# Second feed-forward products as 384 and 192 columns, with the feed-forward steps in the order in which the program traces them

## The chip, the core and the metric

The kernel runs on one core of a Trainium2 chip. A core has five engines with a queue each: TensorE (PE: matrix products, and PEld: the weight loads that go before each product), VectorE (DVE), ScalarE (ACT), GpSimd (POOL) and SyncE (SP, used for DMA issues alone). An engine works through its queue in order, and waits on semaphores for the others. Products write to PSUM, which has eight banks of 128 partitions x 512 float32; everything else works from SBUF.

The metric is the time of the program on the device in microseconds, the median of the runs shown.

## The reference, cut to what matters

Inputs are A_u (1, 2048, 576), the parameters of a state-space convolution (576 channels, 128 states), and the weights w1 (576, 4608) and w2 (4608, 576), all float32.

```
xn  = layernorm(A_u)
ssm = irfft(rfft(xn, 4096) * rfft(K, 4096))[:2048] + xn * Dskip
      K[d, l] = Re sum_n C[d,n] * dt[d] * B[d,n] * exp(dt[d] * A[d,n] * l)
ffn = silu(xn @ w1) @ w2
out = A_u + ssm + ffn
```

The change lies in `ffn`, and there in the second product, `silu(xn @ w1) @ w2`, and in the order of both products on TensorE.

## The kernel before, in words

**Precision.** A float32 product is made of three products of rounded parts (float32r): each operand is split into a high and a low part, and high x high, high x low and low x high are summed in PSUM. ScalarE makes the high part by a copy that rounds, VectorE the low part by a subtraction.

**Feed-forward tiling (`ffn`).** The 2048 tokens are two halves of two blocks of 512. The 4608 hidden units are nine chunks of four tiles of 128. The loop runs over 36 blocks: half, chunk, block of 512 tokens. For a block, `up` (from line 321) computes a tile of 128 hidden units x 512 tokens: 14 products of 512 columns (12 on line 331, one each on lines 332 and 333), then Silu into `gf`, a rounding copy `gh` and the rest `gl` (lines 339 to 342). `down` (from line 344) computes 128 tokens x 576 outputs: the weights of TensorE are 128 tokens of `gh` or `gl`, the moving operand is a part of `w2`. The 576 columns go as two halves of 288 (`HD`), each in a PSUM bank `po` of its own, with 4 tiles x 3 products = 12 products on line 357. After a half VectorE adds the bank to the accumulator `acc[j]` (line 361). There are 144 such steps (36 blocks x 4), with 24 products and two adds each.

**Order.** The program is traced block by block: `u0` of the next block, `d0` to `d3` of this one, `u1`, `u2`, `u3` of the next (the loop over steps at the end of `ffn`), and loads and splits of the next chunk's weights in between (`after`). The order traced is not the order of an engine's queue: a scheduler with a timeline of its own places instructions, and so products of `up` and `down` stand mixed on TensorE. `behind(ins)` (a helper over `tc.issue_after`) tells it to place what follows after an instruction; `tc.high_priority()` puts the adds and the Silu ahead of other work.

**The rest** (`side`, woven between the feed-forward steps by `weave` at shares of the whole): layer norm and transposes of the first 1024 tokens at the start (`phase0`, `normed`, `put_xt`: four transposes a tile on line 124, a copy `xh` on line 125, a subtraction `xl` on line 126; lines 132 to 135 for the last 64 channels), parameters (`natural`), the table of the convolution kernel (`kgen`, VectorE's lines 630 to 676, TensorE's lines 696 and 711, with `spread`, lines 157 to 163), the spectral part (`spectral`, lines 750 to 826), and the inverse (`tail`, `add_conv`, line 847). `marks` (line 865) has the shares at which these begin and end: 0.13 to 0.597 for `kgen`, 0.597 to 0.823 for `spectral`.

**Banks.** PSUM has three pools: `ps1` (two banks) for `up`, `ps2` (three) for `down` and one bank of `add_conv`, `pss` (three) for everything else.

**Weights.** `split_w2` (line 308) loads nothing; it makes `w2h` and `w2l`, each a tile [128, 576] of its own with five buffers, from the loaded `w2r`.

**Start.** Block 0's ups run as two halves of 256 tokens, so that the first 256 tokens are enough to begin; TensorE is kept at work with products of zeros (`idle`, line 879) until then. Tokens 512 to 1023 (block 1, tiles 4 to 7) are normalised and transposed after that.

## Time and profile before

| | |
|---|---|
| median of three runs | 1111.25 us (1109.95 to 1111.63) |
| profiled execution, span from first to last instruction | 1108.2 us |
| profiled execution with what lies around its span | not recorded apart; the median of the runs is 3.05 us above the span |
| TensorE busy (products / weight loads) | 1102.2 us (99%) / 997.5 us (90%) |
| VectorE / ScalarE busy | 916.6 us (83%) / 706.9 us (64%) |
| chain that ended last | TensorE 98%: line 357 42%, line 331 35% |
| granted TensorE clock, mean | 1.000 |

How to read it: a row of a timeline has the start in us from the span's beginning, the time that the merged instructions took together, engine, line of the kernel, operation, tiles written <- tiles read, shape of the weights (TensorE) and of what is written, and how many were merged (x4). In square brackets stands idle time of the engine before it and who ended it. A row of the chain has start, length and the number of instructions. A row of waits has who waited for whom: us in total, times, the longest. Products overlap one another, so a product's own duration (0.29 us for 288 columns) is longer than its distance to the next. An average over the span hides that its stages differ: in slices 6 to 22 of 40 VectorE works on the table of `kgen`, later on the spectral part.

### The profile page before, as it was taken

How to read it: one execution, taken by the hardware profiler on the slowest of the kernel's cores; microseconds unless marked ns; L12 is line 12 of the kernel's file. 1: busy time of each engine (PE TensorE's matmuls, PEld its weight loads, DVE VectorE, ACT ScalarE, POOL GpSimd, SP SyncE). 2: the span in 40 equal slices, each digit the busy share in tenths (PEclk: the TensorE clock that was granted, in tenths of full speed). 3: DMA queues.
4: the chain of work that ended last, by engine and by line, in shares of the span. 5: the costliest groups of instructions: out<-in, count | busy, mean ns of one | idle time of the engine just before them, and what ended most of it. 6: DMA issues, size and time to landing. Idle time of an engine off the chain costs nothing.

```text
span 1108.2 us, 22917 instructions
## 1 busy us (share of the span) xinstructions
PE 1102.2 (99%) x9167; PEld 997.5 (90%) x9167; DVE 916.6 (83%) x1543; ACT 706.9 (64%) x1222; POOL 72.1 (7%) x129
## 2 busy tenths in 40 slices
PE   9999999999999999999999999999999999999998
PEld 7989998899998899899999989999999999999887
DVE  7799899999999999999999737787778778784433
ACT  4564466676677676677867536877777878774210
POOL 1100000000000000011000000000000000000111
PEclk9999999999999999999999999999999999999999
DMA  9745512525252525264744173554544455434983
GB/s 270 190 123 160 152 50 61 120 73 131 77 121 83 116 72 118 77 174 154 206 122 103 45 179 109 162 167 123 156 145 152 138 149 170 129 107 127 241 224 87
DMA packets 175755, 148.56 MB, mean 134 GB/s; under 512 B 111088, under 2 KB 142592, under 8 KB 175520
## 3 DMA queue, kind: packets, MB, share of 16 engines
q1 hardware_dynamic: 165328, 112.63, 38.7%
q0 software_dynamic: 9568, 33.62, 9.6%
q8 instruction: 72, 1.18, 0.5%
q10 hardware_dynamic: 752, 0.85, 0.3%
q14 instruction: 35, 0.29, 0.1%
HBM read 102.53 MB, written 44.61 MB: 133 GB/s over the span
## 4 chain that ended last, share of the span: by engine, by line
PE 98%; DMA 1%; DVE 1%; SPq 0%; issue 0%; DVEq 0%
PE po L357 42%; PE ph L331 35%; PE kp L696 3%; PE ph L332 3%; PE ph L333 3%; PE pu L826 2%; PE pb L826 2%; PE pk L826 2%; PE z L711 2%; PE pu L161 1%; PE py L847 1%; DMA acc<-in_A_u_dram 1%; PE pu L162 1%; PE pt L124 0%; DVE w1l L295 0%; PE ptk L490 0%
## 5 line engine op out<-in xcount | busy, mean ns | idle before, releaser
L357 PE MATMUL po<-w2l,gh 128*128 128x288 f32 x1152 | 338.5, 295 | 0.0
L357 PE MATMUL po<-w2h,gl 128*128 128x288 f32 x1152 | 336.4, 295 | 0.0
L357 PE MATMUL po<-w2h,gh 128*128 128x288 f32 x1152 | 336.1, 295 | 0.0
L357 PEld LDWEIGHTS po<-w2h,gh 128*128 128x128 f32 x1152 | 215.2, 188 | 7.7 <-issue 2.8
L357 PEld LDWEIGHTS po<-w2l,gh 128*128 128x128 f32 x1152 | 215.9, 188 | 5.1 <-issue 0.5
L357 PEld LDWEIGHTS po<-w2h,gl 128*128 128x128 f32 x1152 | 215.4, 188 | 0.9
L339 ACT ACTIVATE gf<-ph 128x512 f32<-128x512 f32 (+1 forms) x148 | 86.4, 584 | 143.8 <-PE ph L333 134.8
L331 PE MATMUL ph<-xh,w1l 128*128 128x512 f32 (+1 forms) x592 | 161.3, 385 | 0.0
L331 PE MATMUL ph<-xh,w1h 128*128 128x512 f32 (+1 forms) x592 | 161.3, 387 | 0.0
L331 PE MATMUL ph<-xl,w1h 128*128 128x512 f32 (+1 forms) x592 | 161.1, 385 | 0.0
L361 DVE TENSOR_TENSOR acc<-po,acc 128x288 f32<-128x288 f32 x288 | 126.2, 451 | 37.0 <-PE po L357 35.6
L342 DVE TENSOR_TENSOR gl<-gf,gh 128x512 fp32r<-128x512 f32 (+1 forms) x148 | 99.0, 672 | 64.6 <-ACT gh L340 63.8
L331 PEld LDWEIGHTS ph<-xh,w1l 128*128 128x128 f32 x592 | 108.0, 188 | 20.0
L331 PEld LDWEIGHTS ph<-xl,w1h 128*128 128x128 f32 x592 | 107.9, 188 | 19.8
L331 PEld LDWEIGHTS ph<-xh,w1h 128*128 128x128 f32 x592 | 104.5, 188 | 16.7 <-ACT x L133 0.5
L340 ACT CAST gh<-gf 128x512 fp32r<-128x512 f32 (+1 forms) x148 | 89.5, 608 | 9.5 <-PE po L357 6.6
L653 ACT ACTIVATE c<-th,magic 128x1040 f32<-128x1040 f32 x36 | 42.1, 1168 | 37.9 <-DVE C L676 28.0
L655 ACT ACTIVATE c<-th 128x1040 f32<-128x1040 f32 x36 | 38.7, 1075 | 33.6 <-DVE th L654 33.6
L314 ACT CAST w2h<-w2r 128x576 fp32r<-128x576 f32 x72 | 47.0, 671 | 17.7 <-PE po L357 14.9
L295 DVE TENSOR_TENSOR w1l<-w1r,w1h 128x640 fp32r<-128x640 f32 x72 | 56.9, 817 | 0.2
L332 PE MATMUL ph<-x,w1h 128*128 128x512 f32 (+1 forms) x148 | 57.0, 386 | 0.0
L333 PE MATMUL ph<-x,w1l 128*128 128x512 f32 (+1 forms) x148 | 56.9, 385 | 0.0
(185 smaller groups left out, 1828.8 us busy)
## 6 DMA issues: line engine op xcount, KB each, us to landing
w2r<-in_B_w_dram SPq DMA_DIRECT2D x72, 288.0 KB, 3.8
w1r<-in_B_w_dram SPq DMA_DIRECT2D x35, 512.0 KB, 3.8
d1u<-u POOLq DMA_DIRECT2D x32, 288.0 KB, 2.5
d1k<-stage SPq DMA_DIRECT2D x18, 512.0 KB, 6.8
ur<-d1u SPq DMA_DIRECT2D x32, 288.0 KB, 3.7
kr<-d1k SPq DMA_DIRECT2D x32, 288.0 KB, 2.9
d<-yo POOLq DMA_DIRECT2D x32, 288.0 KB, 4.0
ys<-d SPq DMA_DIRECT2D x32, 288.0 KB, 11.8
```

The source lines that it names most:

```text
L295: pins["w1l"] = nc.vector.tensor_sub(l1, src, h1).ins
L314: pins["w2h"] = nc.scalar.copy(h2, r2).ins
L331: nc.tensor.matmul(ph, w[:, kt, :], v[:, kt, a:e], start=n + kt == 0, stop=False)
L332: nc.tensor.matmul(ph, h1[:, 4, :], x4[:, a:e], start=False, stop=False)
L333: pins["pe"] = nc.tensor.matmul(ph, l1[:, 4, :], x4[:, a:e], start=False, stop=True).ins
L339: nc.scalar.activation(gf, ph, AF.Silu)
L340: pins["gh"] = nc.scalar.copy(gh, gf).ins
L342: pins["gl"] = nc.vector.tensor_sub(gl, gf, gh).ins
L357: pins["pe"] = nc.tensor.matmul(po[:, :HD], G[blk, t][g][:, js], W2[half, c, t][w][:, hs], start=n == 0, stop=n == 3 * FT - 1).ins
L361: nc.vector.tensor_add(acc[j][:, hs], po[:, :HD], acc[j][:, hs])
L653: nc.scalar.activation(c65, th, AF.Identity, bias=magic)
L826: nc.tensor.matmul(dst, st, mv[:, hs], start=n == 0, stop=n == 3 * len(terms) - 1)
```

## The change

*Columns.* `DA` = 384 and `DB` = 192 take the place of two halves of 288. The first bank of a step takes 12 products of 384 columns. The second bank takes, for each of four tiles, one product of 2 x 192 columns with `gh` as weights: the last 192 columns of the high and of the low part of w2 side by side (so that high x high lands in columns 0 to 191 and high x low in 192 to 383 of the bank), and one of 192 columns with `gl` as weights, which adds low x high to the first 192. On the last tile the two change places. VectorE then makes three adds: 384 columns, and twice 192 into the same columns of `acc`. High and low parts of w2 lie in one tile `w2s` [128, 2, 576] for this.

*Order.* An `up` of whole width is placed behind the last product of the step traced before it (`pins["pe"]`); a step's products for the first bank are placed behind the last product of the step before (`head`), those for the second bank behind the end of the first (`end`). The half-width ups of block 0 keep their rules.

*Marks.* The table work of `kgen` ends, and `spectral` begins, at a share of 0.612 in place of 0.597.

```diff
--- before.py
+++ after.py
@@ -25,6 +25,8 @@
 NJ = 16
 NKT = 4
 HD = D // 2
+DA = 384
+DB = D - DA
 NFT = FF // P
 MAGIC = 12582912.0
 TWO_PI = float(np.nextafter(np.float32(2 * math.pi), np.float32(0)))
@@ -308,15 +310,15 @@
         def split_w2(half, c, t):
             first = half == 0 and c == 0
             r2 = R2.pop((half, c, t))
-            h2 = wp.tile([P, D], F32R, tag="w2h", name="w2h", bufs=FT + 1)
-            l2 = wp.tile([P, D], F32R, tag="w2l", name="w2l", bufs=FT + 1)
+            hl = wp.tile([P, 2, D], F32R, tag="w2s", name="w2s", bufs=FT + 1)
+            h2, l2 = hl[:, 0], hl[:, 1]
             with behind(pins["xt_s"] if first else pins["gh"]):
                 pins["w2h"] = nc.scalar.copy(h2, r2).ins
             with behind(pins["w1l"] if first else None):
                 pins["w2l"] = nc.vector.tensor_sub(l2, r2, h2).ins
             if first and t == 0:
                 pins["w2l0"] = pins["w2l"]
-            W2[half, c, t] = h2, l2
+            W2[half, c, t] = hl
 
         def up(blk, t, a=0, e=512, after=None):
 
@@ -325,6 +327,8 @@
             h1, l1 = W1[half, c, t]
             pool, tag = (ps2, "ps2") if e == 256 and t > 1 else (ps1, "ps1")
             ph = pool.tile([P, 512], F32, tag=tag, name="ph")[:, a:e]
+            if after is None and a == 0 and e == 512:
+                after = pins["pe"]
             for n, (w, v) in enumerate(((h1, xh), (h1, xl), (l1, xh))):
                 for kt in range(NKT):
                     with behind(after):
@@ -348,17 +352,26 @@
             if half == 1 and c == NCH - 1:
                 if jj % 2 == 0:
                     add_conv(j, (acc[j], acc[j + 1]))
-            for h in range(2):
-                hs = slice(h * HD, (h + 1) * HD)
-                po = ps2.tile([P, 512], F32, tag="ps2", name="po")
-                n = 0
-                for t in range(FT):
-                    for g, w in ((0, 0), (0, 1), (1, 0)):
-                        pins["pe"] = nc.tensor.matmul(po[:, :HD], G[blk, t][g][:, js], W2[half, c, t][w][:, hs],
-                                                      start=n == 0, stop=n == 3 * FT - 1).ins
-                        n += 1
+            pa_, pb_ = (ps2.tile([P, 512], F32, tag="ps2", name="po") for _ in range(2))
+            parts = [(*(g[:, js] for g in G[blk, t]), W2[half, c, t], t == 0, t == FT - 1) for t in range(FT)]
+            head = pins["pe"]
+            for gh, gl, w, first, last in parts:
+                with behind(head):
+                    nc.tensor.matmul(pa_[:, :DA], gh, w[:, 0, :DA], start=first, stop=False)
+                    nc.tensor.matmul(pa_[:, :DA], gh, w[:, 1, :DA], start=False, stop=False)
+                    end = nc.tensor.matmul(pa_[:, :DA], gl, w[:, 0, :DA], start=False, stop=last).ins
+            with tc.high_priority():
+                nc.vector.tensor_add(acc[j][:, :DA], pa_[:, :DA], acc[j][:, :DA])
+            both = pb_[:, :2 * DB].rearrange("p (s d) -> p s d", s=2)
+            for gh, gl, w, first, last in parts:
+                with behind(end):
+                    mms = [lambda: nc.tensor.matmul(both, gh, w[:, :, DA:], start=first, stop=last),
+                           lambda: nc.tensor.matmul(pb_[:, :DB], gl, w[:, 0, DA:], start=False, stop=False)]
+                    for mm in mms[::-1] if last else mms:
+                        pins["pe"] = mm().ins
+            for o in (0, DB):
                 with tc.high_priority():
-                    nc.vector.tensor_add(acc[j][:, hs], po[:, :HD], acc[j][:, hs])
+                    nc.vector.tensor_add(acc[j][:, DA:], pb_[:, o:o + DB], acc[j][:, DA:])
             if half == 0 and c == NCH - 1:
                 rows = slice(j * P, (j + 1) * P)
                 nc.sync.dma_start(dr0[rows, :], acc[j])
@@ -862,7 +875,7 @@
 
     def side():
         nonlocal s4, kl, yp, pa, tail_at
-        marks = (0.13, 0.597, 0.823)
+        marks = (0.13, 0.612, 0.823)
         tail_at = (0.91, 0.934, 0.967, 0.0072)
         with tc.tile_pool(name="kf", bufs=1) as kfp:
             for n in ("f", "phi"):
```

## The prediction

> **What bounds the kernel now.** I read the page first (busy times, slices, the chain that ended last), then TensorE's list of waits, then its timeline where one form of product stands alone, and last the first 50 us and VectorE's stretch of kernel-table work.
>
> ```profile
> span 1108.2 us, 22917 instructions
> PE 1102.2 (99%) x9167; PEld 997.5 (90%) x9167; DVE 916.6 (83%) x1543; ACT 706.9 (64%) x1222; POOL 72.1 (7%) x129
> DVE  7799899999999999999999737787778778784433
> PE 98%; DMA 1%; DVE 1%; SPq 0%; issue 0%; DVEq 0%
> ...
> PEld po L357 <- issue: 3.3, 7, 0.5
> ...
> PEld kp L696 <- DVE acc L361: 1.7, 5, 0.4
> ...
> PEld po L357 <- DVE acc L361: 0.4, 1, 0.4
> ```
>
> TensorE is the chain: 98% of it. The waits of its weight loads are a few us in total, those on VectorE about 2 us. So a change is worth what it does to the distance from one product to the next, plus any gap that it opens. VectorE stands at nine tenths in slices 6 to 22, so it is the next bound there.
>
> **The price of a product.** The start of one product to the start of the next is what counts, not the duration of one.
>
> ```profile
> 663.03 3.18 PE po L357 x24
> ...
> 14.07 0.64 PE L331 MATMUL ph<-xh,w1h 128*128 128x256 f32 x4
> ...
> 15.50 0.64 PE L331 MATMUL ph<-xl,w1h 128*128 128x256 f32 x4
> ...
> 800.55 1.07 PE L331 MATMUL ph<-xl,w1h 128*128 128x512 f32 x4
> 801.46 1.07 PE L331 MATMUL ph<-xh,w1l 128*128 128x512 f32 x4
> ...
> 802.59 0.39 PE L333 MATMUL ph<-x,w1l 128*128 128x512 f32 x1
> 802.82 0.29 PE L357 MATMUL po<-w2h,gh 128*128 128x288 f32 x1
> ...
> 301.65 0.29 PE L357 MATMUL po<-w2h,gh 128*128 128x288 f32 x1
> ...
> 301.43 0.19 PEld L357 LDWEIGHTS po<-w2h,gh 128*128 128x128 f32 x1
> 301.65 0.19 PEld L357 LDWEIGHTS po<-w2l,gh 128*128 128x128 f32 x1
> ...
> 501.92 0.19 PEld L161 LDWEIGHTS pu<-sp,s 128*128 128x128 f32 x1
> 502.03 0.19 PEld L162 LDWEIGHTS pu<-sp,s 128*128 128x128 f32 x1
> ```
>
> 288 columns: 3.18/24 = 0.1325 us. 256 columns: 12 in 1.43 us = 0.1192. 512 columns: 4 in 0.91 us = 0.2275. From 288 to 512 that is 0.095/224 = 0.000424 us a column and 0.0104 us fixed; so 384 columns cost 0.1732, and 192, if columns alone counted, 0.0918. A step from one bank to another (802.59 to 802.82, 0.23) costs no more than a step inside one. Loads set a floor: at 501.92 two loads follow each other with nothing ahead of them, 0.11 apart, and only one is drawn ahead: the load for the second product of line 357 starts at 301.65, with the first product, and not when the load of 301.43 was over. A product of 192 columns is over before the next load is, so I price it at 0.11. Its bounds are 0.0918 (columns alone) and 0.1192 (the 256-column row, which a load cannot exceed); the two loads at 501.92 are the nearest row, since they show the load by itself.
>
> [...]
>
> **The change, part by part.**
>
> 1. *Second products.* A step (block, jj) had 24 products of 288: 24 x 0.1325 = 3.180. It now has 12 of 384, four of 384 (both 192s at once) and four of 192: 16 x 0.1732 + 4 x 0.11 = 3.211. 36 blocks x 4 are 144 steps: 144 x 0.031 = **+4.5 us**. Columns streamed are 6912 on both sides. With 192 at 0.0918 it is 144 x -0.042 = -6.0; at 0.1192, 144 x 0.068 = +9.8. That the moving operand of the joint product lies in two pieces has no row; between nothing and one more fixed 0.0104 for each of the 576, +6.0; I take nothing, since the products of one piece in other shapes all fit one line.
>
> 2. *The order written out, at the start.* In the built program TensorE's queue holds all eight half-width first products of block 0, then all 20 transposes of tokens 4 to 7, then up 0 of block 1, and only then the first second product. Before, those filled this time:
>
> ```profile
> 20.00:40.80 20.80, 14.03 (x96) 13.01 (x96) 1.00 0.81 242
> ...
> 30.53 0.29 PE L333 MATMUL ph<-x,w1l 128*128 128x256 f32 x1
> 30.66 0.60 PE L124 MATMUL pt<-ident,xn 128*128 128x128 f32 x4
> ...
> 40.82 2.00 PE L331 MATMUL ph<-xh,w1h 128*128 128x512 f32 x8
> ...
> 46.96 0.39 PE L333 MATMUL ph<-x,w1l 128*128 128x512 f32 x1
> ...
> 26.48 0.79 ACT L339 ACTIVATE gf<-ph 128x256 f32<-128x256 f32 x2 [2.88 <-DVE gl L342]
> ...
> 28.66 0.87 ACT L207 ACTIVATE xn<-acc,mb,sd 128x576 f32<-128x576 f32 x1 [0.80 <-POOL sd L198]
> ...
> 31.29 0.59 ACT L125 CAST xh<-pt 128x512 fp32r<-128x512 f32 x1
> ...
> 27.93 0.57 DVE L202 TENSOR_SCALAR xn<-acc,mv,sd 128x576 f32<-128x576 f32 x1
> ...
> 30.58 1.53 DVE L193 BATCH_NORM_STATS2 st<-xj 128x6 f32<-128x288 f32 x4
> ...
> 32.03 0.67 DVE L126 TENSOR_TENSOR xl<-pt,xh 128x512 fp32r<-128x512 f32 x1
> ...
> 37.65 0.77 DVE L250 STREAM_TRANSPOSE tr<-xj 128x576 f32<-128x576 f32 x1
> ...
> 40.28 0.42 DVE L135 TENSOR_TENSOR x<-pt,x 64x256 fp32r<-64x256 f32 x1
> ```
>
> (The first row is a window of line 357 alone: TensorE's busy time, products, loads, clock.) All 96 second products of block 0 lay between 20 and 40.8 us, and up 0 of block 1 began at 40.82, when its last operand (VectorE's line 135, 40.28 + 0.42) came. What of that chain stays: tokens 4 are normalised at 28.5 (27.93 + 0.57), 5 at 29.5 (28.66 + 0.87), whatever TensorE does. The last half-width up waits for its bank, which the Silu of 26.48 frees: it runs from about 26.9 to 28.6 (14 x 0.1192). Then each of four transposed tiles takes a copy of 0.59 and a subtraction of 0.67, through three banks, behind token 7's normalisation on ScalarE (0.87) and the 1.53 of statistics and other rows on VectorE; the adds of line 361 no longer stand between. Walking the queues by these durations: ScalarE has token 5 done at 29.5, the last Silu, token 7 at 30.6 and the first copy at 31.2; VectorE subtracts to 31.9, which frees the first of the three banks, so token 6's transposes end at 32.5 and its copy at 33.1; the second bank is free at 32.8, token 7's copy is done at 34.2. VectorE has a normalisation (0.57) and a turn (0.77) between, and so subtracts tokens 6 and 7 to 34.4 and 35.7 and the narrow rest to 36.1, 4.6 earlier than before. Up 0's first four products run meanwhile; its last ten end at 38.0. Then 4 steps x 3.211 and one up (14 x 0.2275 = 3.19) bring TensorE to 54.0 with what it had done before at 47.19 (46.96 + 0.23): **+6.8 us**. Bounds: with the operands at 34.0 (nothing but the copies and subtractions in a row) +4.7; at the old 40.7, +11.4. Nothing later gives it back: TensorE has no idle time in the rest of the span.
>
> 3. *The order elsewhere.* Ups come in fours (four times 3.19 us), then four steps of second products. Cover: after up 3 another up (3.19) and the nine products of the first three tiles (9 x 0.1732) stand before the first product that reads up 3's result, 4.7 us, against a Silu, a copy and a subtraction (0.60, 0.62 and 0.69 where these have 512 columns). A bank of second products is wanted again 3.2 us after its last product, as before. I take 0; if VectorE runs behind, it is the second rival.
>
> 4. *VectorE.* One add of 384 and two of 192 replace two of 288.
>
> ```profile
> 407.30 1.29 DVE L342 TENSOR_TENSOR gl<-gf,gh 128x512 fp32r<-128x512 f32 x2
> ...
> 413.66 0.75 DVE L660 TENSOR_TENSOR C<-pw,wb 128x256 f32<-128x256 f32 x2
> ...
> 416.62 1.18 DVE L361 TENSOR_TENSOR acc<-po,acc 128x288 f32<-128x288 f32 x3
> ...
> 144.00:620.00 476.00, 476.00 (x4958) 428.86 (x4957) 461.96 (x692) 331.58 (x499) 20.44 (x37) 1.00 0.41 108
> ...
> 1103.95 0.46 DVE L361 TENSOR_TENSOR acc<-po,acc 128x288 f32<-128x288 f32 x1 [1.14 <-PE po L357]
> ```
>
> In a full queue an add of 288 costs 0.365 (from 1.18 for three), 512 columns 0.60, 256 0.335. So 384 cost 0.47 and 192 0.27: 1.01 a step for 0.73, +0.28. The window (144 to 620, third busy time: VectorE 461.96 of 476) has 14.0 us idle and about 65 steps: +18.2 us. The mark from 0.597 to 0.612 spreads the table work over some 0.015 x 1108 = 16.6 us more. Idle and added stretch together are 30.6, so it fits and costs nothing; without that cover 4.2 us would stick out.
>
> 5. *The rest.* High and low weights share a tile: the same splits, bytes and DMAs, no price. The moved steps issue no DMA but the stores to and loads behind dr0 in chunk 8 of half 0; they keep their place on SP behind the add, and what they bring is read a whole block (25 us) later, and POOL's queue holds none of them. The table work is over later and the spectral part has 0.211 of the steps in place of 0.226; slices 25 to 36 have VectorE at 7 to 8 tenths, so it fits. At the end two adds of 192 follow the last product where one of 288 did (1103.95): +0.2.
>
> Sum: 4.5 + 6.8 + 0.2 = +11.5 us. The profiled execution spans 1108.2 us, 3.05 below the median of the three runs, 1111.25; that distance is what lies around a span and I leave it as it is. 1108.2 + 11.5 + 3.05 = **1122.8 us**.
>
> **The rivals.**
>
> *Not slower: loads are drawn further ahead.* If a 192 costs its columns alone, part 1 is -6.0; with the start at its low bound, +4.7, and 0.2 it is 1110.2. It decides once the gap at the start is under 5.8 us. For it: loads overlap nearly everything (90% busy beside 99%). Against: 301.43 and 301.65. If the start also hides half of its low bound, 1107.8.
>
> *VectorE becomes the bound in the table stretch.* If none of the 14.0 us idle can be used and the longer stretch doesn't help, the 18.2 us are all seen: 1141.0; with the idle time usable but not the stretch, +4.2, 1127.0. For it: 97% busy. Against: TensorE waits about 2 us for VectorE in all.
>
> *The clock falls at the start.*
>
> ```profile
> 1.29 5.11 PE L879 MATMUL pz<-zero 128*128 128x512 bf16 x12 [1.29 <-DVE zero L874]
> ...
> 7.71 1.24 PE L879 MATMUL pz<-zero 128*128 128x512 bf16 x5
> ```
>
> Twelve products of 512 took about 0.42 each at the beginning, five about 0.22 some us later: TensorE begins at half pace. If the two gaps (2.0 and some 3.4 us) bring that back for one up, 14 x 0.2275 = 3.2 more: 1126.0. [...]
>
> *The two-piece operand costs.* +6.0: 1128.8. The change does what it says otherwise: the built queue has each bank's products together.
>
> **How the numbers follow.** Sum as worked out 0.50; the first rival 0.20 (three quarters of it at 1107.8 or lower, as a half hidden start is within the walk's error); VectorE 0.13; clock 0.09; two pieces 0.08. A change under 0.2% (2.2 us, 1109.0 to 1113.5) can't be told from none. The first rival gives faster 0.15 and no change 0.05; to these 0.03 and 0.04 for a walk at the start that is too long: faster 0.18, same 0.09, slower 0.73. The range goes from the low end of the first rival to the clock's and the two pieces' upper ends together with the 192's: 1108 to 1131; below and above it 0.2 are left out. For the sum alone 1116 to 1129.
>
> **What would show it.** Line 357's successors: joint and 384 products 0.173 apart, a 192 followed after 0.11 (after 0.092: first rival). In the first 50 us TensorE idle for about 6 us between 24.9 and 36, ended by tokens 4 to 7. In the table stretch waits of TensorE on line 361's successors stay under 3 us (over 10: second rival). Granted clock 1.0 throughout. Wrong it would be if the gap at the start is not there or other gaps appear at the turn of a chunk.

## The result, and the profile after

The changed kernel takes 1188.2 us (median of four runs, 1185.8 to 1189.4) where the kernel before takes 1110.9: a ratio of 1.0695, 95% interval 1.0681 to 1.0709. That is 77 us slower; 11.5 had been forecast, with 1131 as the upper end. The profiled execution spans 1185.2 us.

The page of the changed kernel: span, busy times, slices of VectorE and the clock, and the chain that ended last.

```profile
span 1185.2 us, 21922 instructions
PE 1128.3 (95%) x8591; PEld 1013.0 (85%) x8591; DVE 960.7 (81%) x1687; ACT 709.9 (60%) x1222; POOL 70.9 (6%) x129
...
DVE  7897989889998989888899964887788888775343
...
PEclk9899999999999999999999999999999999999799
...
PE 61%; DVE 23%; DMA 6%; ACT 5%; issue 4%; SPq 2%; DVEq 0%; POOLq 0%; ACTq 0%
```

TensorE's share of the chain falls from 98% to 61%; VectorE has 23% of it now. Yet VectorE's slices in the table stretch are not fuller than before but emptier (8 and 9 where 9 stood). TensorE's products are busy for 56.9 us less than the span, where before it was 6.0. No engine is full: they wait for one another. The list of waits of the same kernel names the places (who waited for whom: us, times, the longest):

```profile
PE py L860 <- DMA ys<-d: 13.9, 1, 13.9
PEld po L360 <- DVE acc L364: 11.3, 10, 2.1
```

One long wait on a DMA late in the span, and many short ones on VectorE. In the table stretch (busy time of PE, PEld, DVE, ACT, POOL; then clock, DMA share, GB/s):

```profile
144.00:620.00 476.00, 454.67 (x4258) 405.47 (x4257) 431.75 (x683) 300.87 (x448) 18.27 (x33) 0.99 0.38 101
```

From 144 to 620 us TensorE now stands idle for 21.3 us (none before) and VectorE for 44.3 (14.0 before). The same 476 us hold 59 steps in place of 64.

To see where the time goes I take the moment when a step is done, the end of its last add (VectorE reads the bank in PSUM itself and adds it to `acc` in SBUF), and compare steps of the same number, counted from 0. Steps 8 and 128 in the changed kernel, then in the kernel before:

```profile
106.06 0.35 DVE L374 TENSOR_TENSOR acc<-po,acc 128x192 f32<-128x192 f32 x1
...
1065.27 0.74 DVE L374 TENSOR_TENSOR acc<-po,acc 128x192 f32<-128x192 f32 x2
...
1180.79 0.75 DVE L374 TENSOR_TENSOR acc<-po,acc 128x192 f32<-128x192 f32 x2 [0.58 <-PE po L368]
```

```profile
98.05 0.81 DVE L361 TENSOR_TENSOR acc<-po,acc 128x288 f32<-128x288 f32 x2
...
1009.32 0.46 DVE L361 TENSOR_TENSOR acc<-po,acc 128x288 f32<-128x288 f32 x1 [0.57 <-PE po L357]
```

Step 8 is done at 106.4 and not 98.9 (**start: +7.5 us**), step 128 at 1066.0 and not 1009.8 (56.2, of which **+48.7 in the middle**), step 143, the last, at 1181.5 and not 1104.4 (77.1, of which **+20.9 in the tail**). This split into start (to step 8), middle (8 to 128) and tail (128 to 143) is used for every run below. It is read from one profiled execution of each kernel.

The number of a step doesn't say how much other work TensorE has done by then. The products of ups up to the end of step 8, before and changed (length of the window, then busy time and, in brackets, number of the products, of the weight loads and of ScalarE's Silus), and the spectral products of the changed kernel behind step 128:

```profile
0.00:98.86 98.86, 56.38 (x286) 45.94 (x287) 10.20 (x20) 1.00 0.72 191
```

```profile
0.00:106.41 106.41, 45.98 (x238) 38.91 (x238) 8.42 (x17) 0.97 0.69 186
```

```profile
1066.00:1086.00 20.00, 5.73 (x33) 4.98 (x33) 1.00 0.08 30
```

The kernel before has done 48 more products of ups when step 8 is over, 16.4 ups and not 13.0, or 48 x 0.2275 = 10.9 us of work. By step 128 both have done 133.0 ups. So the changed kernel owes 10.9 us at step 8, and it shows in its middle. *By the work done*, that is with these 10.9 us put where the time was lost, its start costs 18.5 us and its middle 37.8. In the same way 33 spectral products of 0.1325 us, 4.4 us, lie in its tail that the kernel before has done by step 128. The table gives the ups done by step 8; 3.19 us for each up fewer than 16.4 go from middle to start.

### The profile page after: what moved, and what is told of

It is laid out like the page before. It is cut to its first block, busy times and chain, and to the rows that moved or that the text cites. A ratio compares the mean times of both kernels' runs of the same rounds, so it can differ in the third digit from the quotient of the medians.

```text
span 1185.2 us, 21922 instructions
## 1 busy us (share of the span) xinstructions
PE 1128.3 (95%) x8591; PEld 1013.0 (85%) x8591; DVE 960.7 (81%) x1687; ACT 709.9 (60%) x1222; POOL 70.9 (6%) x129
## 4 chain that ended last, share of the span: by engine, by line
PE 61%; DVE 23%; DMA 6%; ACT 5%; issue 4%; SPq 2%; DVEq 0%; POOLq 0%; ACTq 0%
PE ph L335 22%; PE po L368 6%; PE po L360 6%; PE po L362 5%; PE po L361 5%; PE po L369 3%; PE pb L839 2%; PE pu L839 2%; PE pk L839 2%; DVE gl L346 2%; DVE S L688 2%; DVE C L677 2%; PE ph L337 2%; PE ph L336 2%; DVE w1l L297 2%
## 5 line engine op out<-in xcount | busy, mean ns | idle before, releaser
L360 PE MATMUL po<-w2s,gh 128*128 128x384 f32 x576 | 198.3, 344 | 14.2 <-DVE acc L364 8.8
L362 PE MATMUL po<-w2s,gl 128*128 128x384 f32 x576 | 195.6, 340 | 5.4 <-DVE gl L346 5.4
L361 PE MATMUL po<-w2s,gh 128*128 128x384 f32 x576 | 195.6, 340 | 0.0
L368 PE MATMUL po<-w2s,gh 128*128 128x384 f32 x576 | 184.3, 355 | 2.7 <-DVE acc L364 2.7
L335 PE MATMUL ph<-xh,w1l 128*128 128x512 f32 (+1 forms) x592 | 158.5, 386 | 0.0
L360 PEld LDWEIGHTS po<-w2s,gh 128*128 128x128 f32 x576 | 109.8, 191 | 23.7 <-DVE acc L364 11.3
L335 PEld LDWEIGHTS ph<-xl,w1h 128*128 128x128 f32 x592 | 109.2, 189 | 21.6
L335 PEld LDWEIGHTS ph<-xh,w1h 128*128 128x128 f32 x592 | 108.1, 189 | 22.2 <-ACT gf L343 3.2
L369 PE MATMUL po<-w2s,gl 128*128 128x192 f32 x576 | 124.9, 256 | 0.0
L362 PEld LDWEIGHTS po<-w2s,gl 128*128 128x128 f32 x576 | 109.7, 190 | 7.0 <-DVE gl L346 7.0
L368 PEld LDWEIGHTS po<-w2s,gh 128*128 128x128 f32 x576 | 108.8, 189 | 4.5 <-DVE acc L364 3.9
L374 DVE TENSOR_TENSOR acc<-po,acc 128x192 f32<-128x192 f32 x288 | 100.7, 354 | 12.7 <-PE po L368 10.1
L361 PEld LDWEIGHTS po<-w2s,gh 128*128 128x128 f32 x576 | 109.7, 190 | 1.4
L369 PEld LDWEIGHTS po<-w2s,gl 128*128 128x128 f32 x576 | 107.0, 189 | 0.0
L364 DVE TENSOR_TENSOR acc<-po,acc 128x384 f32<-128x384 f32 x144 | 79.7, 553 | 23.4 <-PE po L362 22.3
L316 ACT CAST w2s<-w2r 128x576 fp32r<-128x576 f32 x72 | 46.6, 672 | 61.3 <-PE po L369 57.4
```

The source lines that it names most:

```text
L335: nc.tensor.matmul(ph, w[:, kt, :], v[:, kt, a:e], start=n + kt == 0, stop=False)
L360: nc.tensor.matmul(pa_[:, :DA], gh, w[:, 0, :DA], start=first, stop=False)
L361: nc.tensor.matmul(pa_[:, :DA], gh, w[:, 1, :DA], start=False, stop=False)
L362: end = nc.tensor.matmul(pa_[:, :DA], gl, w[:, 0, :DA], start=False, stop=last).ins
L364: nc.vector.tensor_add(acc[j][:, :DA], pa_[:, :DA], acc[j][:, :DA])
L368: mms = [lambda: nc.tensor.matmul(both, gh, w[:, :, DA:], start=first, stop=last), lambda: nc.tensor.matmul(pb_[:, :DB], gl, w[:, 0, DA:], ...
```

## The experiments

Each run is compared with the kernel before on the same chip (1110.2 to 1111.0 us). Times are medians; executions of one changed kernel lay up to 7 us apart (e12). Start, middle and tail are in us against before, from the profiled executions. "Ups" is the number of ups done by step 8. "Lead" says how many steps ahead of the place where it is traced the first product of u1, u2 and u3 stands on TensorE, mean over blocks 5 to 20. "pb done" is the number of steps done when the spectral part's last product ends.

| kernel | time | start | middle | tail | ups | lead u1, u2, u3 | pb done |
|---|---|---|---|---|---|---|---|
| before | 1110.9 | | | | 16.4 | 2.9, 2.4, 1.1 | 129.0 |
| changed | 1188.2 | 7.5 | 48.7 | 20.9 | 13.0 | 0, 0, 0 | 132.2 |
| e1 columns alone | 1153.1 | 14.2 | 15.7 | 13.2 | 17.8 | 4.4, 2.9, 2.4 | 132.3 |
| e2 order alone | 1145.7 | 5.8 | 31.3 | -0.5 | 13.0 | 0, 0, 0 | 128.5 |
| e3 changed, mark 0.597 | 1184.9 | 8.6 | 55.7 | 9.7 | 13.0 | | 131.4 |
| e4 before, mark 0.612 | 1120.0 | 0.4 | 1.7 | 9.1 | 16.4 | 3.0, 1.6, 0.8 | 132.1 |
| e5 e1 with two adds | 1135.3 | 12.1 | 2.0 | 11.2 | 17.7 | 2.8, 2.2, 1.0 | 131.9 |
| e6 before, 320 and 256 | 1119.0 | 4.5 | -1.7 | 7.1 | 17.6 | 2.9, 2.3, 1.1 | 131.4 |
| e7 ups alone pinned | 1150.2 | 0.8 | 39.8 | -0.5 | 13.0 | 0, 0, -0.3 | 128.8 |
| e8 steps alone pinned | 1125.9 | 11.6 | 6.0 | -1.4 | 16.3 | 3.7, 2.5, 1.6 | 128.4 |
| e9 changed, spectral to 0.800 | 1185.4 | 7.9 | 48.3 | 19.0 | 13.0 | | 132.2 |
| e10 e2, ups two steps back | 1148.5 | 8.7 | 30.6 | -0.4 | 13.0 | 1.9, 1.0, 0 | 128.5 |
| e11 e7, less for VectorE | 1148.4 | 0.4 | 38.3 | -0.5 | 13.0 | | 128.8 |
| e12 changed, two adds | 1177.0 | 5.7 | 31.3 | 26.7 | 13.0 | | 132.3 |
| e13 e2 with a lead | 1129.4 | 10.9 | 11.7 | -1.4 | 16.0 | 3.2, 2.2, 0.8 | 128.4 |
| e14 changed with a lead | 1165.4 | 13.0 | 23.0 | 17.4 | 16.0 | 3.7, 2.8, 1.6 | 132.3 |
| e15 changed, py later | 1181.1 | 10.0 | 50.0 | 13.0 | 13.0 | | 132.3 |
| e16 e13, from the second chunk | 1117.1 | -0.4 | 8.5 | -1.4 | 16.0 | 3.3, 2.3, 1.1 | 128.4 |

### Columns alone, order alone, the mark (e1 to e4)

e1 is the changed kernel without its rules of place and with the old mark; e2 the old products with the rules of place (`pins["pe"]` is the last product of the up or step traced before):

```diff
+            if after is None and a == 0 and e == 512:
+                after = pins["pe"]
...
+                head = pins["pe"]
...
+                        with behind(head):
```

> The kernel before with the columns alone: 384 and 192, the joint product, the three adds and the common tile w2s, but no order written out (the scheduler places ups and steps as before) and the mark left at 0.597. Theory A, that the order written out makes the loss (TensorE in a fixed order must wait for VectorE's adds and subtractions, and VectorE in its own fixed order for ScalarE and TensorE): here TensorE always has something else to run, so only the prices of the products and a little more VectorE remain: +2 to +10 us against before (1113 to 1121), TensorE idle under 1%. Theory B, that the three adds make it (more VectorE work than its idle time holds): most of the loss of the stretch from 100 to 683 us stays, +30 to +50 us (1140 to 1160), with VectorE at 97% or more from 144 to 620 us and TensorE waiting on the adds of acc for over 20 us.

> The kernel before with the order alone: halves of 288 and two adds as before, separate tiles for the weights, mark 0.597, but each whole up placed behind the step traced before it and each bank's products behind the bank before. Theory A (the order makes the loss): +45 to +70 us against before (1156 to 1181), with 25 or more gaps of TensorE of about 0.8 to 2 us between 100 and 680 us, and VectorE under 95% in that stretch. Theory B (the three adds make it): only the gap at the start is left, +5 to +12 us (1116 to 1123).

e1: +43 us, ratio 1.038 (1.036 to 1.040). e2: +35.5, ratio 1.032 (1.030 to 1.034). Neither theory holds alone: both parts cost, and their sum (78.4) is the change's loss (77). That holds for the totals alone: the two starts add to 20.0 us against 7.5, the two tails to 12.7 against 20.9. The size of e1 is theory B's, but not its signs, as its row shows: VectorE is at 95% and not 97%.

```profile
144.00:620.00 476.00, 467.31 (x4465) 416.47 (x4467) 453.80 (x714) 311.96 (x471) 19.39 (x35) 1.00 0.39 103
```

e3 and e4 move only `marks` (0.612 to 0.597 in the changed kernel, the reverse in the old one):

> The changed kernel with the mark put back from 0.612 to 0.597, nothing else. The theory of the tail: in the changed kernel the spectral part ends after the feed-forward products have run out, so that the loads of ys are late and TensorE stands 13.5 us and then runs 17 us at half clock. If the mark does this, the spectral part begins about 2 steps (17 us) earlier here, the wait on ys falls under 5 us and the time is 10 to 21 us less than the changed kernel's (1167 to 1178). If instead the table work takes as long as VectorE's and TensorE's waits make it whatever its mark, the time is within 5 us of the changed kernel's (1183 to 1193) and the wait on ys stays over 10 us.

> The kernel before with the mark at 0.612 alone. If the mark by itself costs the tail (the spectral part is squeezed into 0.211 of the steps and cannot be done in them): +10 to +20 us (1121 to 1131), with a wait of TensorE on ys of some us at the end. If the mark is harmless by itself, as the prediction had it: within 3 us of before (1108 to 1114).

e3: 1184.9, 3.3 us less than the changed kernel. The time is that of the second expectation, the tail that of the first: TensorE waits for ys 5.0 us there, 11 us of the tail went, and the middle gave 7 back. e4: +9.85 (ratio 1.009, 1.007 to 1.011), nearly all of it in the tail. The mark is not harmless: alone it costs 9 us after step 128.

### The third add, and a change of size without a change of work (e5, e6)

```diff
-            for o in (0, DB):
+            for o in (0,):
```

> The columns alone (as in the run of the columns alone, which took 43 us more than before), but the third add is left out: the low x high part of the last 192 columns is computed and not added to acc, so that part of the result is missing. VectorE then has one add of 384 and one of 192 a step, about 0.47 + 0.27 = 0.74 us, as much as the two adds of 288 of before (0.73). Theory V (the 43 us come from VectorE's added work, which a stretch with VectorE at 97% cannot hold, and from what follows when it is late): most of it goes, +5 to +15 us against before (1115 to 1125). Theory O (any change to the scheduler's picture of the work gives another order of the queues, and the order of before is one that happens to have no gaps): +30 to +45 us stay (1140 to 1155).

```diff
-            for h in range(2):
-                hs = slice(h * HD, (h + 1) * HD)
+            for hs in (slice(0, 320), slice(320, D)):
```

> The kernel before with the two parts of a step as 320 and 256 columns, nothing else: 12 products at 0.146 and 12 at 0.119 are 3.18 us, as before, and the two adds cost VectorE the same 0.73 us. It is a change of size without a change of work. Theory O (the order of before is the thing that is lost): +10 to +40 us against before (1120 to 1150). Theory V (work is what counts): within 4 us of before (1107 to 1114).

e5 takes 1135.3, between the two theories: without the third add 18 us go, nearly 14 of them in the middle, where the loss falls from 15.7 to 2.0 (by the work done, from 20.0 to 6.1). In its table stretch TensorE has no idle time left:

```profile
144.00:620.00 476.00, 475.94 (x4561) 428.78 (x4560) 455.57 (x681) 325.00 (x491) 20.45 (x37) 1.00 0.41 109
```

The other 24 us of e1 lie mainly in the start and the tail. e6, with neither a product nor an add dearer, costs 8 us, between both expectations: -1.7 in the middle, 4.5 at the start and 7.1 in the tail. At step 8 it has done 1.2 ups more than the kernel before, so by the work done the start is 0.9 and the middle 2.0: nearly all of its loss is the tail. So the middle follows the work, and the tail depends on the order that the scheduler happens to choose.

### Which half of the order (e7, e8)

> Half of the order alone: each whole up is placed behind the step traced before it; the products of a step are left to the scheduler. Halves of 288, mark 0.597. Both halves of the order together took 35.5 us more than before. If the ups, which then stand four in a row, are what takes TensorE its spare work: +20 to +35 us (1130 to 1145) here. If it is the steps in a row (a bank that isn't free yet stops TensorE, where before it ran an up meanwhile): under +10 us (under 1120).

> The other half of the order alone: each bank's second products are placed behind the bank before; the ups are left to the scheduler, which may put them between the banks. If the steps in a row cost the time: +20 to +35 us (1130 to 1145), with TensorE waiting on the adds of acc for over 10 us. If the ups in a row do: under +10 us (under 1120), with waits on acc under 4 us.

e7: +39, 39.8 in the middle. e8: +15, between its two expectations, of it 11.6 by step 8 and only 6.0 in the middle. By the work done e7 is 11.8 at the start and 28.9 in the middle: by step 8 TensorE has stood still for 2.5, 1.5 and 4.7 us, behind adds. So each half of the order costs some 12 us at the start, and what costs the middle is the ups. In e7 TensorE waits for the adds, though nothing was changed in the steps:

```profile
PEld po L359 <- DVE acc L363: 25.3, 20, 4.9
```

```profile
144.00:620.00 476.00, 459.93 (x4567) 412.31 (x4566) 433.37 (x645) 312.28 (x467) 19.36 (x35) 0.99 0.39 101
```

VectorE, which is waited for, is itself busy for only 433.4 of 476 us (462.0 before). The chain that ended last shows what an add waits for. Start, length, engine, tile; x is the number of instructions; TensorE stood idle for 3.22 us before the last row:

```profile
364.63 2.73 PE ph L333 x12
...
367.86 0.61 ACT gf L341
...
369.01 1.35 ACT w1h L293 x2
370.36 0.58 ACT w2h L314
...
371.56 0.70 DVE th L641
...
372.28 1.17 ACT c L655
373.45 0.48 ACT kt L705
...
373.97 0.42 PE z L713 x3
374.38 0.67 DVE C L662 x2
375.06 1.14 DVE C L666
376.19 1.15 DVE th L656
377.34 0.67 DVE C L662 x2
378.01 1.14 DVE C L666
379.15 0.38 DVE acc L363
...
379.57 1.55 PE po L359 x9
```

An up ends, ScalarE does its Silu and then what stands behind it, VectorE goes on with the table, ScalarE copies kt, TensorE does z, VectorE does seven more table instructions, then the add, and then the bank is free. It is one path through the queues of three engines, each worked off in order. TensorE could have done an up meanwhile, but the next one is pinned behind the step that waits.

### Less work for VectorE (e11, e12)

```diff
-                nc.vector.tensor_mul(split(th), row(vt[:, 0:65], 65), col(fT, i, 65))
                 with behind(pins["gl"]):
-                    nc.vector.tensor_add(split(th)[:, :, :, :32], split(th)[:, :, :, :32], col(phiT, i, 32))
+                    nc.vector.tensor_mul(split(th), row(vt[:, 0:65], 65), col(fT, i, 65))
```

> The ups alone pinned (+39 us), with less work for VectorE in the table stretch: the addition of the phase phi to th (36 instructions of 0.68 us, 24.6 us) is left out, so that the table has no phase and the convolution's part of the result is another; its rule of place goes to the multiplication before it. If VectorE's lateness is what TensorE meets (the adds stand in VectorE's queue behind table work that itself waits): -15 to -30 us against the ups alone pinned (1120 to 1135). If the ups in a row cost TensorE by themselves (Silu and its two successors behind each up): within 8 us of 1150 (1142 to 1158).

> The changed kernel without its third add (the low x high part of the last 192 columns isn't added to acc and is missing from the result). With the columns alone this took 18 us away (from +43 to +24). If VectorE's work and the order are two separate losses that add: -14 to -22 us against the changed kernel (1166 to 1174). If the order costs only because VectorE is late (one loss, seen twice): more than 30 us go (under 1158). If the order sets the pace alone: less than 8 (over 1180).

e11: 1148.4, 2 us less than e7, as its second expectation has it in time. But what TensorE waits for is not Silu: the waits on acc stay, with VectorE's load down from 433.4 to 416.8 us in the same window. So this load doesn't make the adds late. That their place in the queue does is what the chain above shows for one add; no run moved the adds alone.

```profile
PEld po L359 <- DVE acc L363: 29.4, 22, 4.3
```

e12 has the edit of e5 in the changed kernel: 1177.0, 11 us less, between two expectations. By stage it is clearer: in the middle 17.4 us go, and what is left there, 31.3, is e2's 31.3; the tail takes 5.8 back. In the middle, order and third add are two losses that add, to within some 6 us: e12's 31.3 hold its dearer products too, and its two executions are 6.8 us apart.

### Giving the ups their lead back (e10, e13, e14, e16)

In the kernel before, u1 begins 2.9 steps before its traced place, u2 2.4, u3 1.1: ups and steps alternate on TensorE. `ends` holds the last product of each step, in the order traced; e10 takes the step two before for all four:

```diff
-                after = pins["pe"]
+                after = (ends or [pins["pe"]])[-3:][0]
```

> The order alone (halves of 288, mark 0.597; +35.5 us with both parts of the order), with one loosening: a whole up is placed behind the step two before the one traced last, so that the scheduler may put ups between the last two steps of a block, where before it did. The ups alone pinned cost +39, the steps alone +15, of which about 12 at the start. If ups are what TensorE runs while it waits for an add of VectorE, and the pinned place takes that away: the loss between steps 16 and 128 (26 to 33 us in the two runs with pinned ups) falls under 12 us and the total to +10 to +22 (1121 to 1133). If any fixed place of the ups costs it: +30 to +42 stays (1141 to 1153).

e10: 1148.5, nothing won; the rival's number. Its leads in the queue are 1.9, 1.0 and 0, so u2, u3 and the next u0 still stand behind the last steps. It leaves open whether the lead or the rule costs. e13 allows more:

```diff
-                after = pins["pe"]
+                after = (ends or [pins["pe"]])[-1 - (1, 4, 4, 3)[t]:][0]
```

> The order alone (halves of 288, mark 0.597, +35.5 us), with the ups placed behind steps further back: u1 and u2 may go up to four steps ahead of where they are traced, u3 three, u0 one; the second products stay bank by bank. In the queue built, the first product of u1, u2, u3 stands 3.2, 2.2 and 0.8 steps ahead of its traced place, against 2.9, 2.4 and 1.1 in the kernel before, 1.9, 1.0 and 0 in the run with ups two steps back (+37.5) and 0 with ups pinned. Theory of the lead (what costs is that ups come late and in a row, so that TensorE has four steps in a row, each bank waiting for its add, and then four ups in a row, each waiting for Silu): the loss between steps 8 and 128, 31 us in both those runs, falls under 10 us, total +8 to +22 us (1119 to 1133). Rival (a rule of place as such misleads the scheduler, whatever lead it allows): the loss between steps 8 and 128 stays over 25 us, total +30 to +42 (1141 to 1153).

> The changed kernel with the same loosening of the ups (up to four, four, three steps ahead; u0 one); columns, the order of the banks and the mark 0.612 stay. Leads in the queue built: 3.7, 2.8 and 1.6 steps. Theory of the lead: of the 49 us that the changed kernel loses between steps 8 and 128, about 31 go and the 15.7 us of the columns alone stay, total +40 to +55 us against before (1151 to 1166). Rival: within 8 us of the changed kernel (1180 to 1196).

e13: 1129.4 (+19); the middle falls from 31.3 to 11.7, a little over the 10 expected. Half of that fall is work that e13 has done by step 8 and e2 owes; by the work done the middle falls from 20.3 to 10.3 and the start from 16.8 to 12.3. e14, the same line in the changed kernel: 1165.4, 23 us less than it; the middle falls from 48.7 to 23.0 (by the work done, from 37.8 to 21.6). Both totals are the lead theory's. A rule that leaves the ups 3.2, 2.2 and 0.8 steps of lead costs about half of one that leaves them none (19.1 of 35.5 us).

e16 is e13 with `and (half or c)` in the condition of the ups and `head` None in the first chunk:

> The order with the lead of the ups (which took 19 us more than before), left out for the first chunk: ups and steps of the first two blocks are where the scheduler puts them. The prediction had the order cost 6.8 us at the start, since TensorE waits for the transposes of tokens 4 to 7 with nothing else placed ahead of them; after step 8 the runs with the order of the steps were 6 to 12 us late. If that is so: the loss at step 8 goes from 10.9 us to under 2 and the total to +8 to +13 us (1118 to 1124). If the loss at the start is not the order's: at step 8 still over 6 us, total within 4 us of 1129.

e16: 1117.1 (ratio 1.006, 1.004 to 1.008). The start's 10.9 us are gone (-0.4), so in e13 that loss was the order of the first two blocks. TensorE has 95% of the chain again:

```profile
PE 95%; DVE 2%; DMA 1%; ACT 1%; issue 0%; DVEq 0%
```

### The tail (e9, e15)

In the changed kernel the spectral part's last product is followed by one store of `yo`, loads of `ys`, and then `py`, the inverse's first product. Timeline, changed kernel:

```profile
1084.97 0.29 PE L839 MATMUL pb<-yh,mm 128*128 128x288 f32 x1
...
1086.26 0.54 POOL L792 DMA_DIRECT2D d<-yo  x1 [7.19 <-ACT yo L791]
...
1091.24 0.39 PE L337 MATMUL ph<-x,w1l 128*128 128x512 f32 x1
...
1091.73 1.28 SPq L848 DMA_DIRECT2D ys<-d  x2
...
1105.56 2.20 PE L860 MATMUL py<-ys,s 64*32 64x288 f32 x32 [13.93 <-DMA ys<-d]
...
1108.18 0.52 PE L361 MATMUL po<-w2s,gh 128*128 128x384 f32 x1
1108.50 0.52 PE L362 MATMUL po<-w2s,gl 128*128 128x384 f32 x1
```

TensorE runs out of work at 1091.6 and waits for data that lands 10 to 14 us after its issue; then its products stand 0.32 apart in place of 0.173, at a half clock that began in the idle time (granted clock 0.5 from 1094.7 to 1111.7). From pb's end to py it is 20.3 us: a copy, the store, the issue of the loads, their landing. In the kernel before pb ended at 1009.9, py came at 1032.0, and 3.6 steps with the ups among them lay between. The table has the pattern: all runs with pb done at step 129.0 or before lose nothing in the tail, all with pb at 131.4 or later 7 to 27 us; py stands at step 132.6 to 132.9 in all but e15.

```diff
-        marks = (0.13, 0.612, 0.823)
+        marks = (0.13, 0.612, 0.8)
```

> The changed kernel with the mark at which the spectral part is to be done at 0.800 in place of 0.823, nothing else. In the kernel before, the last product of the spectral part (pb) ends at the 129.0th of 144 steps, in the changed one at the 132.2th, and the first product of the inverse (py) stands on TensorE at step 132.7 in both; the loads of ys between the two land after 11 us. Runs with pb done by step 129.0 had no loss after step 128, runs with pb at 131.4 or later 7 to 21 us. If that is the tail: pb is done about 3 steps earlier here (step 129 to 130), the wait on ys is under 2 us and the time from step 128 to the end falls by 12 to 20 us: 1168 to 1177. If the tail has another cause, the time stays within 5 us of the changed kernel's: 1183 to 1193.

```diff
-        tail_at = (0.91, 0.934, 0.967, 0.0072)
+        tail_at = (0.91, 0.95, 0.967, 0.0072)
```

> The changed kernel with the first products of the inverse (py) moved later, from a share of 0.934 to 0.950 of the steps; nothing else. The mark of the spectral part did not move its end in the queue (step 132.2 with 0.823 and with 0.800), so the other end of the wait is moved: py comes about two steps later, at step 135, while the loads of ys start where they did. If TensorE has run out of work between the end of the spectral part and py: the wait of 13.9 us on ys and the half clock behind it are gone, 12 to 20 us less than the changed kernel: 1167 to 1177. If the time is needed anyway (the inverse's own adds and stores set the end): within 5 us of it (1183 to 1193).

e9 missed: pb stays at 132.2 and the time at 1185.4. The end mark of the spectral part doesn't set its end. e15: py is at step 136.1, the wait before its first product is gone, and 7 us go (1181.1), 7.9 in the tail; that is between both expectations. The next loads of ys are late then (5.1 us). So the first wait is shown as the cause of some 8 of the 21 us. The rest can be counted in the traces: the changed kernel's tail has the 13.9 us of idle time, 6.2 us of products at half clock, which cost 3.1, and 4.4 us of spectral products that the kernel before has behind it; that is 21.4 for 20.9. In e15 the same three are 5.1, 3.0 and 4.4, or 12.5 for 13.0. That leaves next to nothing for the inverse's own length. Why the scheduler ends the spectral part three steps later with every change to the columns and with the mark, and not with rules for ups or steps alone, was not found.

No kernel here beats the one before.

## Why the prediction was right or wrong

1. **Second products, +4.5: right in its prices, a third too small.** A step of 20 products in a row is shown here from its first product to the one that follows it, 900.04 to 903.26. Over all such stretches at full clock the median is 3.227 us, and 3.181 for 24 products before: +0.046 a step, 6.6 us in all, inside the bounds of -6.0 and +9.8. (The 32 steps from 96 to 128 took 264.6 us, before 263.6, which is the forecast's +0.031 a step; that is luck, since other runs with the same products took 260.8 to 264.8 there.) Products and then loads of the changed kernel:

```profile
900.04 0.34 PE L360 MATMUL po<-w2s,gh 128*128 128x384 f32 x1
...
902.38 0.36 PE L368 MATMUL po<-w2s,gh 128*128 128x384 f32 x1
902.58 0.25 PE L369 MATMUL po<-w2s,gl 128*128 128x192 f32 x1
902.67 0.36 PE L368 MATMUL po<-w2s,gh 128*128 128x384 f32 x1
...
903.26 0.29 PE L839 MATMUL pu<-uh,mm 128*128 128x288 f32 x1
```

```profile
902.30 0.19 PEld L368 LDWEIGHTS po<-w2s,gh 128*128 128x128 f32 x1
902.41 0.19 PEld L369 LDWEIGHTS po<-w2s,gl 128*128 128x128 f32 x1
902.58 0.19 PEld L368 LDWEIGHTS po<-w2s,gh 128*128 128x128 f32 x1
```

A pair takes 0.29 by the products (902.38 to 902.67) and 0.28 by the loads: 0.173 + 0.11. Two loads follow each other after 0.11, so the price of a load holds. The two-piece operand can cost no more than the 2.1 us by which the forecast was short (4 ns a product), and not the rival's 6.0. The first rival (loads drawn further ahead) and the fourth (two pieces) are out.

2. **The start, +6.8: right in cause, about half the size.** The walk ended with up 1 of block 1, at 54.0 in place of 47.19. Up 1 ended at 59.71, where up 2 begins: +12.5. Taking the order out of the first chunk took the whole start loss of e13 away (e16). TensorE's timeline in the changed kernel:

```profile
27.59 0.74 PE L335 MATMUL ph<-xh,w1h 128*128 128x256 f32 x4 [2.04 <-ACT gf L343]
30.26 0.66 PE L126 MATMUL pt<-ident,xn 128*128 128x128 f32 x4 [0.29 <-ACT xn L209]
32.48 0.66 PE L126 MATMUL pt<-ident,xn 128*128 128x128 f32 x4 [1.35 <-DVE xl L128]
33.48 1.12 PE L126 MATMUL pt<-ident,xn 128*128 128x128 f32 x4 [0.34 <-DVE xl L128]
35.27 2.07 PE L335 MATMUL ph<-xh,w1h 128*128 128x512 f32 x4 [0.25 <-ACT xh L127]
...
40.75 0.33 PE L360 MATMUL po<-w2s,gh 128*128 128x384 f32 x1
...
55.24 0.44 PE L368 MATMUL po<-w2s,gh 128*128 128x384 f32 x1 [1.52 <-DVE acc L364]
...
59.71 1.07 PE L335 MATMUL ph<-xh,w1h 128*128 128x512 f32 x4
```

Up to 36 us it is idle for 2.04 + 0.29 + 1.35 + 0.34 + 0.25 = 4.3 us, ended by the Silu and by tokens 4 to 7, not for the 6 forecast, and the clock rival came true beside it: half clock from 33.1 to 40.0 us (the four products at 35.27 take 2.07, in full clock 1.07). Up 0 is done at 40.75 and not at 38.0. The four steps then take 15.75 us, to 56.50, and not 12.84: TensorE waits for an add, and twelve products of the parameters (0.9 us), which before came after 47.19, stand between. The walk had no add that comes late. Two more gaps of 2.2 us follow, at 79 and 104 us, and by step 8 the start has cost 18.5 by the work done. That the adds of step 8 show +7.5, near the forecast, is luck. In the columns alone the start costs 14.2 (9.8 by the work done) without any rule of place, from another order of the queues; so it is not a term of the order alone.

3. **The order elsewhere, 0: this step failed.** The order alone costs 35.5 us (e2), 20.3 of them in the middle by the work done. I asked whether each up's result is ready before it is read, 4.7 us of cover, and whether a bank is wanted again sooner, 3.2 us as before. By the durations both answers stand as long as nothing is late; the term was put at 0 on that. Missing was what TensorE has to do *while* it waits: before, ups ran up to three steps ahead and lay between the steps. Pinned, they leave four steps in a row, each bank of which waits for an add whose place in VectorE's queue is behind work that waits for ScalarE and TensorE. e13 and e14 give the lead back and get 16 and 23 us.

4. **VectorE, 0: this step failed too, with its rival's price near.** The third add costs 17.4 us in the middle of the changed kernel and 13.7 in the columns alone; 18.2 was the price if none of the idle time could be used. The step took VectorE's idle time for room. The mark's longer stretch gave 7.0 us of cover in the middle (e3: 55.7 without it) and cost 11.2 in the tail. The second rival, at 0.13, was right in that the idle time gave no room, and its sign came (over 10 us of waits on the adds: 11.3). But VectorE did not become the bound: it is busy for 431.75 of 476 us, less than before, and 16.6 us less load gave 2 us (e11). The third add stands between a bank's last product and its release, which the table work dropped in e11 does not; that this is the difference was not tested.

5. **The rest, "so it fits" and +0.2: failed**, at 21 us. I set the spectral part's share of the steps against VectorE's tenths; what counts is the distance between its last product and the inverse's first on TensorE, 3.6 steps before and 0.6 after, against a way of some 20 us from the one to the other, 11 of them the loads. The mark alone costs 9 us there in the kernel before (e4).

By stage the 77.1 us are 18.5 at the start, 37.8 in the middle and 20.9 in the tail, by the work done. By kind TensorE's idle time grew by 50.9 us (56.9 for 6.0), the half clock cost 11.3 (22.6 us of work in it), the dearer products 6.6; some 8 us show as none of these. The forecast's sum had the first two of its terms in the right place and too small, and called the large ones nothing. Its upper end, 1131, holds the clock's 3.2 and the 192's 5.3 but not the two pieces' 6.0 that it names (1137.3 with them), nor the second rival's own 1141.0. The sentence "wrong it would be if other gaps appear at the turn of a chunk" did not name their place either: gaps of 0.2 us and more come in 15 of the 18 blocks from 2 to 19, where the table work runs, and in none from 20 to 31.

## What to carry to other kernels

Before an order is written out, measure in the trace how far work runs ahead of its traced place: that lead is what an engine does while it waits for another, and here a rule that took it away cost time although every single dependence had cover. An engine's idle time inside a stretch where it is 97% busy was not room for more work. When two orders are compared at a milestone, count the work that each has done by then: here 10.9 us that were lost before step 8 showed only behind it. And where a load must land between two stages, count the work that lies between them on the bound engine: here 3.6 steps were enough and 0.6 was not, and small edits far away, even one to the width of a product, moved that distance.

## What the runs showed of the hardware

Short gaps can cost twice. In the changed kernel's trace, from 20 us on, TensorE (no product and no load) has 23 gaps of 0.8 us and more. Three of 2.03, 2.02 and 2.14 us, which end at 323.10, 449.33 and 524.20, were each followed within 0.5 us by 3.41 us at granted clock 0.5 (from 323.26, 449.55 and 524.64). The gap of 13.9 us before py had 0.5 from 3.1 us after its beginning (1094.67), for 17.07 us in all. Three of 2.04, 2.21 and 2.19 us, which end at 27.59, 81.66 and 106.52, were followed by none within 5 us. Of the sixteen from 0.8 to 1.8 us one was followed by half clock, the one of 1.34 that ends at 32.48: 6.83 us from 33.12. These are the five stretches that the changed kernel has before its end, 34 us in all, 17 of them about the wait on ys. In 3.41 us full of work half the clock costs 1.7 us, nearly as much again as the gap of 2 us before it. By these rows the length of a gap alone doesn't tell: 2.02 us had half clock behind it and 2.21 had not, and what decides it was not shown. The kernel before, which from 20 us on has no gap of over 0.2 us, was granted 1.00 over all of 20 to 1108.2 us.

A wide product's recorded start says less than its load's. After a joint product the 192 starts 0.20 later and the next joint product 0.09 after that (902.38, 902.58, 902.67), while the loads stand 0.11 and 0.17 apart (902.30, 902.41, 902.58); only the sum of a pair can be read from the products.
